# A transformer step in one kernel: no weight tasks in a unit's short last block, and a pace of 54 slots in place of 58

## The chip, the cores and the metric

The kernel runs on one core of a Trainium2 chip. The metric is the time of one execution on the device, in microseconds (us). A core has a matmul engine (PE), a vector engine (DVE), a scalar engine (ACT), GpSimd (POOL) and SyncE (SP), which here issues most of the DMAs. Each engine works off its own list of instructions in order; semaphores make one wait for another.

## The reference

Attention with a block mask feeds a layer of 8 experts with soft weights, and that feeds a gated layer:

```
attn = softmax(mask(q k^T / 8)) v                 # 4 batches x 8 heads, 576 positions of 64
x = attn as 2304 rows of 512
P = exp(x w_gate - max); 8 times: rows and columns of P are normed in turn
out = sum over e of P[:, e] * (relu(x w1[e]) w2[e])      # 8 experts, 512 -> 1024 -> 512
result = (silu(out wg) * (out wv)) wo                    # 512 -> 1536 -> 512
```

## The kernel before, in words

The experts are worked off as 16 units (half of an expert's hidden width each). The 2304 rows lie in two halves of 1152, and every product of a unit is done by a scheme of seven products of blocks in place of eight (Strassen's, in Winograd's form), each of them in three f16 products of high and low parts. A half's 1152 rows are cut in blocks of 256, 256, 256, 256 and 128, so a unit has four full blocks and a short one (`blocks`, `NB` = 5, `TB` = 256).

`products_in` issues the seven products of a block into three PSUM banks a, b and c in the order b c b a b c b. It yields after every half product: a full block takes 14 slots, a short one 7 (a short block's product is not halved). One `yield` is one slot of the planner. In the slot the main loop (`for _ in in_stream()`) also pulls one piece of an output product (`products_out`, lines 632 to 670, evacuated by ACT at lines 1427 and 1447 through `take`), and calls `background()`. The fifth product, S3, leaves its sum in bank b, where DVE's add of line 559 reads it; the seventh, X22, is written to the same bank, so PE waits for that add. DVE's adds of line 704 and subtractions of lines 193 and 680 make the low and high parts of the hidden activations (`sums_out`, `operand`), ACT's casts of line 683 the high parts.

Background tasks prepare the weights: those of the next expert unit (`expert_items`) and a share of those of the gated layer (`glu_items`). A task is some instructions: a maximum (line 375 or 437, DVE), a spread of it over the partitions (line 103 on DVE, 110 on PE, 116 on DVE) and the scale behind it (lines 155 to 163), a split in high and low parts (line 178 on ACT and 182 on DVE) with a subtraction of two quarters (line 303, DVE). They are queued in `bg`, and `bg.step()` issues one, or two light ones. `bg.load` fetches the next item's data ahead of it.

`background()` is asked once a slot. `todo` is the count of tasks left; `pace` holds the count at the unit's start and the slot it was taken in; `late` is `todo` less what a straight line down to zero would have left. Two tests follow each other, so up to two steps may be made in a slot: a step is made if `late` is above `most`, or above `-ahead` while `given`, a running sum of DVE work, is low. What is left at a unit's end stands in the queue when the next unit adds its own; `bg.until` forces tasks out if the weights a unit needs aren't made.

What is called a unit's first, second, third or fourth block below are its full ones. Tasks in a short block stand on DVE and ACT between the block's own instructions, in the order in which the slots issue them.

Of the kernel before, what the change touches and what calls it, by code (L numbers as in the profile page):

```python
# [30 lines left out]
def attention_moe_glu_kernel(  # L31
# [37 lines left out]
    TB = 256  # L69
    NU = E * FF // FU  # L70
    NG = F2 // FU
    blocks = [(c, min(TB, NH - c)) for c in range(0, NH, TB)]
# [435 lines left out]
    def later(d, f):  # L508

        due.setdefault(clock[0] + d, []).append(f)  # L510
# [160 lines left out]
    def operand(h, o, name, n, src, func=AF.Copy):  # L671

        h[o] = places.take(f"{name}_h{o}")
        hi, lo, src = h[o][:, 0, :, :n], h[o][:, 1, :, :n], src[:, :, :n]
        if func == AF.Relu:
            nc.scalar.activation(hi, src, AF.Relu)  # L676

            def cut_lo():
                given[0] += n
                nc.vector.scalar_tensor_tensor(lo, src, 0.0, hi, op0=ALU.max, op1=ALU.subtract)  # L680

            return cut_lo
        nc.scalar.copy(hi, src)  # L683
        if o in POOL_LO:
            return lambda: nc.gpsimd.tensor_tensor(lo, src, hi, op=ALU.subtract)

        def plain_lo():
            given[0] += n
            half_lo(lo, src, hi)

        return plain_lo
# [3 lines left out]
    def sums_out(h, name, n, x11, x12, x21, x22, spare, relu):  # L695


        los = {}

        def plus(o, x, y, op):  # L700
            o, x, y = (z[:, :, :n] for z in (o, x, y))
            given[0] += n
            if relu:
                nc.vector.scalar_tensor_tensor(o, x, 0.0, y, op0=ALU.max, op1=op)  # L704
            else:
                nc.vector.tensor_tensor(o, x, y, op=op)

        def step1():
            plus(spare, x22, x21, ALU.add)
            plus(x21, x11, x21, ALU.subtract)  # L710
            places.give(x22)

        def step2():
            los[S1] = operand(h, S1, name, n, spare)
            los[S3] = operand(h, S3, name, n, x21)
            plus(x11, x11, spare, ALU.subtract)

        def step3():
            los[S1]()
            los[S3]()  # L720
            places.give(spare, x21)
            los[S2] = operand(h, S2, name, n, x11)
            plus(x12, x12, x11, ALU.add)

        def step4():
            los[S2]()
            places.give(x11)
            los[S4] = operand(h, S4, name, n, x12)

        def step5():  # L730
            los[S4]()
            places.give(x12)

        for d, f in enumerate((step1, step2, step3, step4, step5)):
            later(d + 2, f)
# [3 lines left out]
    def expert_in(u, b, bank):  # L739

        h = hts[u, b] = {}
        n = blocks[b][1]
        name = f"m{u}_{b}"
        q = {}

        def plain(t, half, src, spare):
            h[t, half] = places.take(f"{name}_h{t}{half}")
            hi, lo = h[t, half][:, 0, :, :n], h[t, half][:, 1, :, :n]
            s = src[:, :, :n]
            if spare is not None:  # L750
                places.give(spare)

            def first():
                nc.scalar.activation(hi, s, AF.Relu)
                later(1, rest)

            def rest():
                nc.vector.scalar_tensor_tensor(lo, s, 0.0, hi, op0=ALU.max, op1=ALU.subtract)  # L758
                if (t, half) != (1, 0):
                    places.give(src)  # L760

            if (t, half) == (1, 1):
                later(3 if n == TB else 1, first)
            else:
                first()

        def quad(t, half, src, spare):
            q[t, half] = src
            if spare is not None:
                q["spare"] = spare  # L770
            if (t, half) == (1, 0):
                r = places.take(f"{name}_r", F32)
                nc.scalar.activation(r[:, :, :n], src[:, :, :n], AF.Relu)
                sums_out(h, name, n, q[0, 0], q[0, 1], r, q[1, 1], q["spare"], True)
                return
            o = {(0, 0): X11, (0, 1): X12, (1, 1): X22}[t, half]
            later(3 if o == X22 and n == TB else 2, lambda: later(1, operand(h, o, name, n, src, AF.Relu)))

        yield from products_in(name, b, units[u][0], bank, plain if u < 2 else quad, b == NB - 1)
# [481 lines left out]
    with tc.manual_schedule():  # L1261
# [123 lines left out]
        slots, ready_at, outs = [0], {}, set()  # L1385
# [69 lines left out]
        def out_stream(items, make):  # L1455

            for it in items:
                while ready_at.get(it, slots[0] + 1) > slots[0]:
                    yield False
                yield from make(*it)  # L1460
                outs.add(it)

        def in_stream():
            for u, b in seq:
                if u and b == (NEARLY if u < 2 else 0):
                    bg.until((u, 0))
                    if 2 <= u < NU - 1:
                        n = -(-sum(len(i[2]) for i in glu) // (NU - 1 - u))
                        share = []
                        while glu and n >= len(glu[0][2]) * 0.6:  # L1470
                            share.append(glu.popleft())
                            n -= len(share[-1][2])
                        if u == NU - 2:
                            share.extend(glu)
                            glu.clear()
                        i1, i2 = expert_items(u + 1)
                        bg.add(share[:-2] + [i1] + share[-2:] + [i2])
                        pace[:] = [sum(len(i[2]) for i in bg.items) + len(bg.now), slots[0]]
                yield from expert_in(u, b, bank)
                ready_at[u, b] = slots[0] + LAG  # L1480

# [150 lines left out]
        def glu_out(t, b):  # L1632
            def take(i, tk, cols, ps, what=None):
                if tk is None:
                    return
                x = tk * NI + i
                a = acc[:, x, cols]
                first = t == 0 and (x, cols.start) not in begun
                begun.add((x, cols.start))
                if first:  # L1640
                    nc.scalar.activation(a, ps, AF.Copy, scale=sos[b][:, t : t + 1])
                else:
                    nc.vector.scalar_tensor_tensor(a, ps, sos[b][:, t : t + 1], a, op0=ALU.mult, op1=ALU.add)
                count[x] = count.get(x, 0) + 1
                if count[x] == 3 * NG:
                    for g in range(4):
                        r0 = (4 * i + g) * CB + tk * HB
                        nc.sync.dma_start(out[r0 : r0 + HB, :], acc[g * HB : (g + 1) * HB, x])

            yield from products_out(f"go{t}_{b}", b, hts.pop((t, b)), gw[t, "o"], m, mdone, take, b == NB - 1)  # L1650
# [4 lines left out]
        def prep_stream():  # L1655
            for b in range(NB):
                while (NU - 1, b) not in outs:
                    yield False
                yield from x2_prep(b)
                prepped.add(b)  # L1660
# [9 lines left out]
        prepped = set()  # L1670
        seq3 = seq + [(NU + t, b) for t in range(NG) for b in range(NB)]
        xstream = prep_stream()
        pace = [0, 0]
        ostream = out_stream(seq3, lambda u, b: expert_out(u, b) if u < NU else glu_out(u - NU, b))
        credit = [0]

# [6 lines left out]
        def background():  # L1683


            given[0] = max(0, given[0] - 480)
            for ahead, room, most in ((6, 200, 6), (-2, 100, 11)):
                todo = sum(len(i[2]) for i in bg.items) + len(bg.now)
                late = todo - pace[0] * (1 - (slots[0] - pace[1]) / 58)
                if late > most or late > -ahead and given[0] < room:  # L1690
                    bg.step()

        for _ in in_stream():
            slots[0] += 1
            pull(1)
            if slots[0] % 2 == 0:
                next(steps, None)
            if routed and unscaled and (unscaled[0] % NI * P < blocks[NEARLY][0] or (1, NB - 1) in outs):
                scale_acc()
            next(xstream, None)  # L1700
            background()
            if len(made) == 2 * NU and places.spare(1):
                load_next()
# [50 lines left out]
```

## Time and profile before

| | us |
|---|---|
| median of 3 runs | 2087.34 |
| lowest and highest | 2084.76, 2088.24 |
| span of the profiled execution | 2083.4 |
| PE busy | 1949.0 (94%) |
| DVE busy | 1620.1 (78%) |
| ACT busy | 1379.9 (66%) |

The profile gives the execution's span, from its first to its last instruction, and no other time of it. The attention part ends before 400 us, the expert units run to about 1660, and the gated layer to the end. In the expert units PE is busy for 90% or more of every slice, and DVE between 80% and 90% of most.

### The profile page before, as it was taken

Reading aid. Unit: us, or ns where it says so; the run is one execution under the profiler, and the core shown is the slowest. Engines: PE = TensorE matmul, PEld = TensorE weight load, DVE = VectorE, ACT = ScalarE, POOL = GpSimd, SP = SyncE. Lnnn points to the kernel's source line nnn. Section 1 sums busy time; section 2 is a strip of 40 time slices with the busy share of each in tenths; the row PEclk is TensorE's granted clock in tenths of the full one; section 3 lists DMA queues with packets and bytes.
Section 4 is the critical chain, followed back from the end, with each engine's and each line's share of the span. In section 5 each row is a group of like instructions: output and inputs, shape, how many; then the busy total and the mean of one; then the engine's idle time right before and its main releaser. Section 6 shows DMA issues by size and latency. Waiting matters only on the chain.

```text
span 2083.4 us, 47251 instructions
## 1 busy us (share of the span) xinstructions
PE 1949.0 (94%) x18378; PEld 1672.9 (80%) x18378; DVE 1620.1 (78%) x3455; ACT 1379.9 (66%) x2940; POOL 612.8 (29%) x873
## 2 busy tenths in 40 slices
PE   6789899799999999999999999999999988999998
PEld 3457676698888888888888888888888877988887
DVE  7887765668787887978878788888887877666666
ACT  5665766348777777878777777777776566544442
POOL 4534444102333333333332333333332123000000
PEclk9889999999999999999999999999999999999999
DMA  5433331306687866878668786777877100301112
GB/s 155 112 96 105 84 105 49 122 22 122 120 172 155 172 136 125 178 150 171 132 132 179 149 178 134 153 157 144 180 148 168 37 11 1 87 21 37 47 42 52
DMA packets 168721, 236.41 MB, mean 113 GB/s; under 512 B 16432, under 2 KB 85680, under 8 KB 168496
## 3 DMA queue, kind: packets, MB, share of 16 engines
q0 software_dynamic: 66560, 107.37, 30.8%
q1 hardware_dynamic: 101936, 126.01, 19.9%
q8 instruction: 144, 2.36, 0.5%
q14 instruction: 81, 0.66, 0.1%
HBM read 90.98 MB, written 24.38 MB: 55 GB/s over the span
## 4 chain that ended last, share of the span: by engine, by line
PE 55%; DVE 15%; ACT 5%; DMA 3%; issue 3%; SPq 0%; POOL 0%; ACTq 0%; DVEq 0%
PE abc_m_b L537 11%; PE m_o_b L645 11%; PE m_o_ac L645 8%; PE abc_m_c L537 5%; PE abc_m_a L537 3%; PE abc_v_b L537 3%; PE abc_g_b L537 3%; PE m_go_b L645 3%; PE m_go_ac L645 2%; DVE m_t L704 2%; DVE m_h L193 2%; DMA wr<-in_w_dram 2%; PE abc_v_c L537 1%; DVE w L182 1%; PE abc_g_c L537 1%
## 5 line engine op out<-in xcount | busy, mean ns | idle before, releaser
L537 PEld LDWEIGHTS <-w 128*128 128x128 f16 x6720 | 609.8, 98 | 110.9 <-issue 45.7
L645 PEld LDWEIGHTS <-m_h 128*128 128x128 f16 x5292 | 514.0, 98 | 69.0 <-issue 10.5
L537 PE MATMUL abc_m_b<-xs,w 128*128 128x256 f16 (+1 forms) x3840 | 476.6, 264 | 31.9 <-DVE m_t L559 29.4
L1443 POOL DMA_DIRECT2D acc<-ev x351 | 305.4, 895 | 581.3 <-ACT ev L1447 367.4
L645 PE MATMUL m_o_b<-w,m_h 128*128 128x256 f16 x3024 | 403.5, 273 | 7.9 <-ACT ev L1447 7.7
L645 PE MATMUL m_o_ac<-w,m_h 128*128 128x256 f16 x2268 | 309.4, 273 | 0.4 <-ACT ev L1447 0.4
L537 PE MATMUL abc_m_c<-xs,w 128*128 128x256 f16 (+1 forms) x1920 | 230.7, 263 | 2.2 <-DVE m_h L758 1.6
L1447 ACT ACTIVATE ev<-m_o_b,pe 128x256 f32<-128x256 f32 x351 | 161.7, 476 | 64.0 <-PE m_o_b L645 52.8
L1447 ACT ACTIVATE ev<-m_o_ac,pe 128x256 f32<-128x256 f32 (+1 forms) x234 | 135.7, 580 | 47.8 <-PE m_o_ac L645 46.4
L178 ACT ACTIVATE w<-wr,ws 128x512 f16<-128x512 f32 x210 | 150.5, 723 | 12.7 <-DVE ws L163 10.3
L182 DVE SCALAR_TENSOR_TENSOR w<-wr,ws,w 128x512 f16<-128x512 f32 x210 | 155.5, 747 | 1.4 <-ACT w L178 1.4
L1431 POOL DMA_DIRECT2D acc<-ev_s x65 | 73.6, 1132 | 259.1 <-ACT ev_s L1427 259.1
L683 ACT CAST m_h<-m_t 128x512 f16<-128x512 f32 (+1 forms) x210 | 121.8, 580 | 41.2 <-DVE m_t L704 40.3
L676 ACT ACTIVATE m_h<-m_t 128x512 f16<-128x512 f32 (+1 forms) x210 | 121.8, 582 | 35.8 <-DVE m_t L574 24.9
L193 DVE TENSOR_TENSOR m_h<-m_t,m_h 128x512 f16<-128x512 f32 (+1 forms) x210 | 133.1, 635 | 8.7 <-ACT m_h L683 8.4
L680 DVE SCALAR_TENSOR_TENSOR m_h<-m_t,m_h 128x512 f16<-128x512 f32 (+1 forms) x210 | 132.2, 635 | 5.8 <-ACT m_h L676 5.6
L537 PEld LDWEIGHTS <-gg_w 128*128 128x128 f16 x1260 | 113.5, 98 | 22.2 <-issue 10.7
L996 POOL TENSOR_SCALAR e<-e,r 128x64 f32<-128x64 f32 (+2 forms) x144 | 78.1, 548 | 166.8 <-DVE r L991 111.9
L645 PEld LDWEIGHTS <-g_h 128*128 128x128 f16 x1134 | 111.0, 99 | 18.9 <-issue 5.4
L537 PEld LDWEIGHTS <-gv_w 128*128 128x128 f16 x1260 | 113.6, 98 | 13.2 <-issue 1.7
L537 PE MATMUL abc_m_a<-xs,w 128*128 128x256 f16 (+1 forms) x960 | 117.5, 262 | 0.0
L375 DVE TENSOR_REDUCE wmx<-wr 128x1 f32<-128x512 f32 x128 | 85.7, 679 | 15.0 <-DMA wr<-in_w_dram 14.9
(298 smaller groups left out, 3364.0 us busy)
## 6 DMA issues: line engine op xcount, KB each, us to landing
acc<-ev POOLq DMA_DIRECT2D x351, 256.0 KB, 4.3
wr<-in_w_dram SPq DMA_DIRECT2D x128, 256.0 KB, 4.8
acc<-ev_s POOLq DMA_DIRECT2D x52, 256.0 KB, 4.3
st<-hl SPq DMA_DIRECT2D x48, 144.0 KB, 3.6
raw_g<-in_w_gate_dram SPq DMA_DIRECT2D x12, 512.0 KB, 5.5
raw_v<-in_w_val_dram SPq DMA_DIRECT2D x12, 512.0 KB, 4.5
raw_o<-in_w_out_dram SPq DMA_DIRECT2D x12, 512.0 KB, 5.0
scr_g<-gg SPq DMA_DIRECT2D x21, 256.0 KB, 2.9
```

Of the source, the lines that this page charges most:

```text
L178: nc.scalar.activation(hi, src, AF.Copy, scale=s)
L182: nc.vector.scalar_tensor_tensor(lo, src, s, hi, op0=ALU.mult, op1=ALU.subtract)
L193: nc.vector.tensor_sub(lo, src, hi)
L375: nc.vector.tensor_reduce(g["mx"][:, k : k + 1], g["b"][k // 2][k % 2], axis=AX.XY, op=ALU.max, apply_absolute_value=True)
L537: nc.tensor.matmul(ps[:, f], W[o][:, sh, k, f * P : (f + 1) * P], xs[:, o, mh, k, c0 : c0 + n], start=x not in begun, stop=True, skip_grou ...
L645: nc.tensor.matmul(ps, h[o][:, sh, k, ii * P : (ii + 1) * P], W[o][:, mh, k], start=o in (X11, X12) and k == 0 and j == 0, stop=True, skip ...
L676: nc.scalar.activation(hi, src, AF.Relu)
L680: nc.vector.scalar_tensor_tensor(lo, src, 0.0, hi, op0=ALU.max, op1=ALU.subtract)
L683: nc.scalar.copy(hi, src)
L996: nc.gpsimd.tensor_scalar(et[c][:, :n], et[c][:, :n], g["r"][:, c : c + 1], 1.0, op0=ALU.mult, op1=ALU.mult)
L1443: nc.gpsimd.dma_start(acc[:, x], e, accum_op=ALU.add)
L1447: nc.scalar.activation(e[:, cols], ps, AF.Copy, scale=p)
```

## The change

`short[0]` is set when a unit's block is begun, true for the block of 128 rows; `background()` returns at once while it is true. The straight line of the pace reaches zero 54 slots after the unit's start, and not 58. Nothing else differs, and no instruction is new.

```diff
--- before.py
+++ after.py
@@ -1476,6 +1476,7 @@
                         i1, i2 = expert_items(u + 1)
                         bg.add(share[:-2] + [i1] + share[-2:] + [i2])
                         pace[:] = [sum(len(i[2]) for i in bg.items) + len(bg.now), slots[0]]
+                short[0] = blocks[b][1] < TB
                 yield from expert_in(u, b, bank)
                 ready_at[u, b] = slots[0] + LAG
 
@@ -1670,7 +1671,7 @@
         prepped = set()
         seq3 = seq + [(NU + t, b) for t in range(NG) for b in range(NB)]
         xstream = prep_stream()
-        pace = [0, 0]
+        pace, short = [0, 0], [False]
         ostream = out_stream(seq3, lambda u, b: expert_out(u, b) if u < NU else glu_out(u - NU, b))
         credit = [0]
 
@@ -1684,9 +1685,11 @@
 
 
             given[0] = max(0, given[0] - 480)
+            if short[0]:
+                return
             for ahead, room, most in ((6, 200, 6), (-2, 100, 11)):
                 todo = sum(len(i[2]) for i in bg.items) + len(bg.now)
-                late = todo - pace[0] * (1 - (slots[0] - pace[1]) / 58)
+                late = todo - pace[0] * (1 - (slots[0] - pace[1]) / 54)
                 if late > most or late > -ahead and given[0] < room:
                     bg.step()
```

The first place is DVE's list in the short block of unit 6 (its weight tasks are unit 7's, `w_7`), around the add of line 559 into which bank b (`abc_m_4_b`; 4 is the block) is summed. Before:

```order
L193 TENSOR_TENSOR m_3_h_12550<-m_3_t_12348,m_3_h_12550 128x512
L182 SCALAR_TENSOR_TENSOR w_7_0_12532<-wr_1_00_12300,ws_1_12523,w_7_0_12532 128x512
L303 TENSOR_TENSOR wr_1_00_12300<-wr_1_01_12302,wr_1_00_12300 128x512
L182 SCALAR_TENSOR_TENSOR w_7_1_12554<-wr_1_10_12304,ws_1_12523,w_7_1_12554 128x512
L303 TENSOR_TENSOR wr_1_01_12302<-wr_1_11_12306,wr_1_01_12302 128x512
L559 TENSOR_TENSOR m_4_t_12609<-m_4_t_12506,abc_m_4_b 128x2x128
L193 TENSOR_TENSOR m_3_h_12571<-m_3_t_12317,m_3_h_12571 128x512
L574 TENSOR_TENSOR m_4_t_12546<-m_4_t_12546,abc_m_4_c 128x2x128
```

After:

```order
L704 SCALAR_TENSOR_TENSOR m_3_t_12351<-m_3_t_12351,m_3_t_12274 128x512
L193 TENSOR_TENSOR m_3_h_12525<-m_3_t_12274,m_3_h_12525 128x512
L193 TENSOR_TENSOR m_3_h_12527<-m_3_r,m_3_h_12527 128x512
L704 SCALAR_TENSOR_TENSOR m_3_t_12320<-m_3_t_12320,m_3_t_12351 128x512
L193 TENSOR_TENSOR m_3_h_12554<-m_3_t_12351,m_3_h_12554 128x512
L559 TENSOR_TENSOR m_4_t_12605<-m_4_t_12523,abc_m_4_b 128x2x128
L193 TENSOR_TENSOR m_3_h_12573<-m_3_t_12320,m_3_h_12573 128x512
```

One pair of 182 and 303 is left out here, and the other has moved to an earlier place, ahead of the block before's three 704s; `w_7_1` is made in unit 7.

The second place is DVE's list in the fourth block of unit 7, around its add of line 559 (`abc_m_3_b`). The `gv` are splits of the gated layer's weights. Before:

```order
L103 TENSOR_SCALAR w_d<-ident,wm_8_1_13628 128x128
L182 SCALAR_TENSOR_TENSOR gv_2_13605<-f_v_11_13399,gs_v_13533,gv_2_13605 128x512
L303 TENSOR_TENSOR f_v_11_13399<-f_v_11_13399,f_v_00_12309 128x512
L182 SCALAR_TENSOR_TENSOR gv_4_13625<-f_v_00_12309,gs_v_13533,gv_4_13625 128x512
L303 TENSOR_TENSOR f_v_10_13338<-f_v_10_13338,f_v_11_13399 128x512
L559 TENSOR_TENSOR m_3_t_13694<-m_3_t_13565,abc_m_3_b 128x512
L680 SCALAR_TENSOR_TENSOR m_3_h_13675<-m_3_t_13654,m_3_h_13675 128x512
L182 SCALAR_TENSOR_TENSOR gv_6_13664<-f_v_01_12885,gs_v_13533,gv_6_13664 128x512
L182 SCALAR_TENSOR_TENSOR gv_5_13686<-f_v_11_13399,gs_v_13533,gv_5_13686 128x512
L574 TENSOR_TENSOR m_3_t_13616<-m_3_t_13616,abc_m_3_c 128x512
L182 SCALAR_TENSOR_TENSOR gv_3_13707<-f_v_10_13338,gs_v_13533,gv_3_13707 128x512
```

After:

```order
L193 TENSOR_TENSOR m_2_h_13576<-m_2_t_13331,m_2_h_13576 128x512
L182 SCALAR_TENSOR_TENSOR gv_2_13562<-f_v_11_13382,gs_v_13495,gv_2_13562 128x512
L303 TENSOR_TENSOR f_v_11_13382<-f_v_11_13382,f_v_00_12266 128x512
L182 SCALAR_TENSOR_TENSOR gv_4_13596<-f_v_00_12266,gs_v_13495,gv_4_13596 128x512
L303 TENSOR_TENSOR f_v_10_13323<-f_v_10_13323,f_v_11_13382 128x512
L182 SCALAR_TENSOR_TENSOR gv_6_13635<-f_v_01_12936,gs_v_13495,gv_6_13635 128x512
L182 SCALAR_TENSOR_TENSOR gv_5_13653<-f_v_11_13382,gs_v_13495,gv_5_13653 128x512
L559 TENSOR_TENSOR m_3_t_13702<-m_3_t_13573,abc_m_3_b 128x512
L680 SCALAR_TENSOR_TENSOR m_3_h_13683<-m_3_t_13661,m_3_h_13683 128x512
L182 SCALAR_TENSOR_TENSOR gv_3_13673<-f_v_10_13323,gs_v_13495,gv_3_13673 128x512
L116 TENSOR_REDUCE w_r<-m_w_13663 128x1
```

Two splits, `gv_6` and `gv_5`, stand ahead of the add where they stood behind it. The short block's add of this unit is the same row of DVE's list before and after.

## Rows read from the trace of the kernel before

**Rows 1.** The page's head, and PE's granted clock in 40 slices (tenths).
```profile
span 2083.4 us, 47251 instructions
...
PEclk9889999999999999999999999999999999999999
```

**Rows 2.** Windows: span, busy PE, PEld, DVE, ACT, POOL (instructions), clock, DMA share, GB/s.
```profile
935.10:955.20 20.10, 18.45 (x166) 15.91 (x164) 19.68 (x38) 16.63 (x33) 6.50 (x8) 1.00 0.78 172
956.50:967.60 11.10, 9.63 (x128) 8.75 (x126) 10.82 (x24) 10.52 (x24) 3.47 (x4) 1.00 1.00 207
...
1041.90:1052.80 10.90, 9.46 (x128) 8.82 (x127) 10.69 (x19) 9.86 (x22) 3.47 (x4) 1.00 0.74 123
...
1107.80:1126.10 18.30, 18.30 (x170) 16.39 (x169) 16.38 (x28) 13.81 (x28) 6.35 (x8) 1.00 1.05 255
```

**Rows 3.** Table of waits: engine, line, waited for, us in total, times, longest.
```profile
PE abc_m_b L537 <- DVE m_t L559: 29.4, 15, 6.2
```

**Rows 4.** Timeline (start, length, engine, line, idle before): PE's waits, units 0, 2, 14.
```profile
396.33 3.71 PE L537 MATMUL abc_m_b<-xs,w 128*128 128x256 f16 x24 [6.17 <-DVE m_t L559]
...
412.11 0.83 PE L537 MATMUL abc_m_b<-xs,w 128*128 128x128 f16 x12 [3.67 <-DVE m_t L559]
...
534.29 0.83 PE L537 MATMUL abc_m_b<-xs,w 128*128 128x128 f16 x12 [1.81 <-DVE m_t L559]
...
1571.14 0.83 PE L537 MATMUL abc_m_b<-xs,w 128*128 128x128 f16 x12 [1.34 <-DVE m_t L559]
```

**Rows 5.** Timeline of PE and DVE in unit 6's short block.
```profile
874.21 0.83 PE L537 MATMUL abc_m_b<-xs,w 128*128 128x128 f16 x12
...
875.72 0.74 DVE L182 SCALAR_TENSOR_TENSOR w<-wr,ws,w 128x512 f16<-128x512 f32 x1
...
876.20 0.82 PE L645 MATMUL m_o_ac<-w,m_h 128*128 128x256 f16 x6
...
876.50 0.69 DVE L303 TENSOR_TENSOR wr<-wr,wr 128x512 f32<-128x512 f32 x1
...
877.11 0.74 DVE L182 SCALAR_TENSOR_TENSOR w<-wr,ws,w 128x512 f16<-128x512 f32 x1
...
877.77 0.68 DVE L303 TENSOR_TENSOR wr<-wr,wr 128x512 f32<-128x512 f32 x1
...
878.37 0.41 DVE L559 TENSOR_TENSOR m_t<-m_t,abc_m_b 128x256 f32<-128x256 f32 x1
...
878.71 0.68 DVE L193 TENSOR_TENSOR m_h<-m_t,m_h 128x512 f16<-128x512 f32 x1
...
878.84 0.83 PE L537 MATMUL abc_m_b<-xs,w 128*128 128x128 f16 x12 [1.82 <-DVE m_t L559]
```

**Rows 6.** Timeline of DVE, ACT and PE in unit 13's fourth block.
```profile
1457.72 0.75 DVE L182 SCALAR_TENSOR_TENSOR go<-f_o,gs_o,go 128x512 f16<-128x512 f32 x1
...
1458.39 0.69 DVE L303 TENSOR_TENSOR f_o<-f_o,f_o 128x512 f32<-128x512 f32 x1
...
1459.59 0.69 DVE L193 TENSOR_TENSOR m_h<-m_r,m_h 128x512 f16<-128x512 f32 x1
...
1460.19 0.69 DVE L704 SCALAR_TENSOR_TENSOR m_t<-m_t,m_t 128x512 f32<-128x512 f32 x1
...
1460.91 0.62 ACT L683 CAST m_h<-m_t 128x512 f16<-128x512 f32 x1 [1.80 <-DVE m_t L704]
...
1461.44 0.83 ACT L1447 ACTIVATE ev<-m_o_b,pe 128x256 f32<-128x256 f32 x2
...
1461.95 0.82 PE L645 MATMUL m_o_b<-w,m_h 128*128 128x256 f16 x6 [1.75 <-ACT ev L1447]
```

**Rows 7.** Timeline of PE and DVE in unit 7's fourth block.
```profile
945.68 0.82 PE L645 MATMUL m_o_b<-w,m_h 128*128 128x256 f16 x6 [0.99 <-ACT ev L1447]
...
950.31 0.46 PE L110 MATMUL m_w<-w_d,ones 128*128 128x128 f32 x2 [0.54 <-DVE w_d L103]
...
952.73 0.68 DVE L559 TENSOR_TENSOR m_t<-m_t,abc_m_b 128x512 f32<-128x512 f32 x1
...
953.88 0.82 PE L537 MATMUL abc_m_b<-xs,w 128*128 128x256 f16 x6
```

## The prediction

> **What bounds the kernel now.** I read the page's busy shares first, then the table of waits, then the timeline of TensorE (PE) alone, and last the timeline of all engines around each gap. From about 440 to 1640 us the kernel runs the expert units, and there TensorE is the bound: the granted clock stands at its highest digit in every slice after the first four [rows 1] (1.00 in blocks of units 7 to 9, so the 2.4 GHz level), and a full block of 14 slots takes 18.30 us in which PE is busy for all 18.30 [rows 2], so a slot is 1.31 us. Time is lost only where PE stands still. The table of waits has one entry that is large and repeats: PE's products into bank b waiting for the vector engine's (DVE's) add of line 559, 15 times, 29.4 us together [rows 3]. Two of the 15 lie in unit 0, 6.17 and 3.67 us. The other 13 are one per unit, units 2 to 14, always before the last product of the short block, 1.81 us in the first and 1.34 in the last [rows 4]; together 29.4 - 6.17 - 3.67 = 19.6 us. In order they are 1.81, 1.81, 1.34, 1.43, 1.82, 1.34, 1.43, 1.82, 1.34, 1.44, 0.80, 1.80 and 1.34.
>
> How one comes about is seen in unit 6 [rows 5]. The fifth product (S3) starts at 874.21 and lasts 0.83, so its sum can be added from about 875.1. DVE gets to the add at 878.37, since from 875.72 it works off two pairs of weight tasks, 182 and 303, that stand ahead of it in its order. PE's work before the seventh product ends at 876.20 + 0.82 = 877.02, and the product starts at 878.84. Without the two pairs the add would start at 875.72 and PE would find it done. In the short block a slot is no longer than elsewhere, but product and add follow two slots apart in place of four or five. The room is 877.02 - 875.1 less the add's 0.41, 1.5 us of queue on DVE; in a full block it is one slot more, less the longer add, 2.6.
>
> **What a queue is made of.** An instruction on 512 columns is shown as 0.69 us long, a 182 as 0.75, but the next starts 0.60 and 0.67 us after it [rows 6], and after a 256-column add 0.34. I count with these steps: I went through DVE's order slot by slot, added the steps and took 1.31 off per slot; what is left over is the queue. On the kernel before this gives 1.7 to 3.7 us of queue ahead of the short block's add, so 0.2 to 2.2 us of wait against 0.80 to 1.82 measured. That is good to about half a microsecond, one unit apart: unit 3, where it gives least and 1.81 was measured, since DVE stood waiting for a transfer there.
>
> The Trainium skill speaks to this choice: "Perfetto Trace Analysis", section "Per-instruction lifecycle", says that the shown window of a DVE instruction runs until its write is acknowledged, while the next may start to fetch when the execution is over. By the shown lengths the short blocks of before would have waited 2 to 3 us each, near twice what was measured, so the steps stand.
>
> **The change, part by part.** No instruction is added or taken away; tasks move. (1) In the short block no weight task is issued, so DVE's work there falls from 10.5 to 12.1 us (by steps, in 9.17 us of slots; the trace shows 10.69 and 10.82 busy in units 8 and 7 [rows 2]) to 6.0. (2) The 7 or 8 tasks go into the four full blocks, through the pace of 54 slots, and 8 or 9 tasks of a unit's supply (1 to 5 before) are left for the next unit's first block. That block, in units 3 to 14, had DVE at 53 to 61% by steps and gets 62 to 69%: it costs nothing. None is left for the forced loop at a unit's start or at its first output: both find their weights made.
>
> The units fall into three kinds that repeat.
> - Units 2, 5, 8, 11: the full blocks' DVE load stays at or below 0.90 of the slots; the queue ahead of the short add falls from 3.0 (unit 2: 3.7) to 0.5 us, below 1.5. Their waits go: 1.81 + 1.43 + 1.43 + 1.44 = 6.1 us.
> - Units 3, 6, 9, 12, 13: the third block rises from 0.83-0.90 to 0.97 (13: 1.02), but the queue is drained before the short add, 0.2 to 0.4 us, in unit 13 1.6. Their waits (1.81 + 1.82 + 1.82 + 0.80 + 1.80) go but for 0.1: 7.9 us.
> - Units 4, 7, 10, 14: the second block comes to 1.04 and the fourth, 1.04 before, to 1.09. The short add stands behind as much work as before (it is the same row of DVE's order), with 2.7 us of queue against 2.6. Their four waits of 1.34 stay.
>
> **What the moved tasks cost.** PE waits in full blocks by another way, seen in unit 13 [rows 6]: DVE's queue delays the 704 at 1460.19, the scalar engine (ACT), in order, waits 1.80 for it with its cast of line 683, behind that cast stands the evacuation of line 1447, and PE's next output product waits for that one, 1.75 us. The queue there, at the second or fourth block's start, was 5.1 us; unit 9 had 3.3 at that place and lost nothing. Interpolated: nothing below 3.3, one us more of wait per us of queue. After the change the queue there is 4.0 to 4.3 in units 3, 6 and 9: 0.7 each, 2.1. In unit 13 it is 5.2, as before, and a second place at 4.2 adds 0.9. In the kind of unit 7 it is 4.2 once and 3.9 once: 0.9 + 0.6; these units had already 0.99 and 0.54 [rows 7], and their fourth block's add, which had 953.88 - 952.73 - 0.68 = 0.47 us to spare [rows 7], now stands behind two more 182s (1.33) and takes perhaps 0.4. But a stall of PE lets DVE catch up, and so the short block's wait shrinks by about what the earlier ones grew; I take their sum, 2.87 per unit, as unchanged (from 1.3 less to 2.5 more, times four). Bounds for all of these places: from 0 (unit 9 before) to 1.75 (unit 13 before) each. I take 2.1 + 0.9 = 3.0.
>
> **Unit 0 and 1.** The short block of unit 0 has four pairs and three maxima ahead of its add, some 6.9 us, all moved out: 3.67 us go. They land in unit 1's first block: 19 tasks where 7 were, a queue of about 3 us, over the 2.6 for line 559 by 0.4 and in front of the last relu (line 758), whose bank the next block's product wants a slot later, some 2 us; nothing like it was lost there before. Bounds 0 and 3.7; I take 2.4, a net gain of 1.3.
>
> **Sum.** 6.1 + 7.9 - 3.0 + 0 + 1.3 = 12.3 us off the profiled span of 2083.4 us, so 2071.1. The page gives no time of that execution beside its span; the three timed runs are 2084.76 to 2088.24, so about 4 us lie around the span or between executions. I take the 12.3 off the median: 2075.0 us. The attention part before and the gated part after it hold the same instructions in the same order; the first block of unit 15 gets four tasks more at a DVE load of 0.62.
>
> **Rivals.**
> - All cover holds: the queues drain a little faster than I count (half a microsecond, the error above), no new wait arises, and the four 1.34s shrink too. Ceiling 19.6 + 3.7 = 23 us: 2064. For it: DVE often waits for PE in full blocks of before; against: fourth blocks over 1.0. Chance 0.12.
> - Half of it is given back: new waits of 1.2 to 1.7 at the ten or so places: 4 to 8 us saved, 2079 to 2083. Chance 0.16.
> - The waits only move: if an instruction held DVE for its whole shown length (0.69 and 0.75), DVE would be over 1.0 in nearly every third and fourth block, the four short adds would wait 2.8 us more each (11 us), and gain and loss cancel: 2083 to 2091. Against it: the counted waits of before. Chance 0.14.
> - Slower: the in-order ACT chain of unit 13 (683 behind 704, 1447 behind both) at all twelve places where DVE's queue rises over 3.3, with the queue at each passing its 5.1: 12 x 1.75 = 21 plus 2.4 in unit 1, against 6.1 + 7.9 + 3.7 = 17.7 gained: 5.7 us more, 2093. It decides if the queue there passes 5 us, 0.8 to 1.2 above my count. Chance 0.07.
> - The change doesn't do what it says, the tasks being forced in one burst at the unit's start: the order shows them spread over the first block, so 2087; chance 0.01.
>
> **The numbers.** The forecast, 2071 to 2079, has 0.50. A difference below 0.2% (4.2 us) can't be told from none. Faster: 0.50 + 0.12 + 0.16 = 0.78; same 0.14; slower 0.08. The range for 8 in 10 is 2068 to 2086: it leaves out most of the ceiling and the slower case; the forecast's own range is 2071 to 2079.
>
> **What would show it.** Right: PE's waits for line 559 fall from 15 to about 6, 29.4 us to about 12 (6.17 of unit 0 stays); the short blocks of units 2, 3, 5, 6, 8, 9, 11 and 12 last 9.2 us; units 4, 7, 10 and 14 still wait there or, for the same sum, earlier. New waits for line 1447 of under 1 us stand near the fourth block's start of units 3, 6 and 9. Wrong: waits of PE for line 1447 or line 559 in full blocks that sum to over 10 us, or short blocks that still wait in the first two kinds.

## The result and the profile after

The change made the kernel slower: 2111.9 us against 2086.1 (medians), a ratio of 1.0123 (95% interval 1.0109 to 1.0137), about 26 us. One of the four timed runs of the changed kernel was slow (4040 us) and stands outside the ratio, though it counts in this median; the other three took 2110.85 to 2112.87. The forecast was 2075, its range for 8 in 10 ended at 2086, and its slowest rival stood at 2093. The profiled execution has a span of 2109.1 us where [rows 1] has 2083.4, so its 25.7 us are the same loss, and it can be read from the trace.

The page's head of the changed kernel, and the granted clock in 40 slices:

```profile
span 2109.1 us, 47276 instructions
...
PEclk9889999899999999999999999999999999999999
```

From its table of waits (engine, line, waited for, us in total, times, longest):

```profile
PE abc_m_b L537 <- DVE m_t L559: 28.9, 11, 5.7
...
DVE wmx L375 <- DMA wr<-in_w_dram: 17.2, 13, 3.4
PE m_o_b L645 <- ACT ev L1447: 17.0, 18, 1.7
...
ACT f_o L456 <- DMA raw_o<-in_w_out_dram: 11.2, 3, 5.2
ACT f_v L456 <- DMA raw_v<-in_w_val_dram: 11.1, 3, 4.6
...
ACT f_g L456 <- DMA raw_g<-in_w_gate_dram: 9.2, 3, 5.1
```

PE's wait for line 559 is as long in sum as in [rows 3], and that hides everything: none of the 13 short blocks waits for it any more, and eight full blocks do, 2.03 to 3.70 us each, 21.9 together. Line 1447 went from 7.7 us to 17.0. The four rows of DVE and ACT are the ones that the prediction left out: they wait for loads (DMA). Before, the same rows were a fifth shorter in sum, and that of line 1447 less than half as long:

```profile
DVE wmx L375 <- DMA wr<-in_w_dram: 14.9, 12, 3.9
...
ACT f_v L456 <- DMA raw_v<-in_w_val_dram: 8.7, 3, 3.8
...
ACT f_o L456 <- DMA raw_o<-in_w_out_dram: 8.2, 3, 4.2
...
PE m_o_b L645 <- ACT ev L1447: 7.7, 11, 1.8
...
ACT f_g L456 <- DMA raw_g<-in_w_gate_dram: 7.5, 3, 4.7
```

Two kinds of load are meant. A weight item of an expert is fetched by four DMAs into `wr`, and its first tasks are the four maxima of line 375. A gated item is fetched as 64-bit words into the tile `raw`, which has one buffer; ACT reads it in line 456, DVE shifts the result in line 461 and reads `raw` again up to line 471, and only then can the next `raw` load start.

What matters is what stands behind the waiting instruction in its engine's order. Unit 9's fourth block, changed kernel, timeline (start, length, engine, line, idle before):

```profile
1133.34 2.68 SPq L370 DMA_DIRECT2D wr<-in_w_dram  x4
...
1137.26 0.69 DVE L375 TENSOR_REDUCE wmx<-wr 128x1 f32<-128x512 f32 x1 [0.90 <-DMA wr<-in_w_dram]
...
1140.26 2.02 DVE L375 TENSOR_REDUCE wmx<-wr 128x1 f32<-128x512 f32 x3 [2.31 <-DMA wr<-in_w_dram]
...
1142.71 0.68 DVE L559 TENSOR_TENSOR m_t<-m_t,abc_m_b 128x512 f32<-128x512 f32 x1
...
1143.44 0.82 PE L537 MATMUL abc_m_b<-xs,w 128*128 128x256 f16 x6 [2.85 <-DVE m_t L559]
```

All four maxima stand ahead of the add, DVE idles 0.90 and 2.31 us for the transfer, and PE waits 2.85. The same place before:

```profile
1118.07 1.97 SPq L370 DMA_DIRECT2D wr<-in_w_dram  x4
...
1121.67 0.69 DVE L375 TENSOR_REDUCE wmx<-wr 128x1 f32<-128x512 f32 x1 [1.05 <-DMA wr<-in_w_dram]
1122.28 0.68 DVE L559 TENSOR_TENSOR m_t<-m_t,abc_m_b 128x512 f32<-128x512 f32 x1
...
1124.81 0.69 DVE L375 TENSOR_REDUCE wmx<-wr 128x1 f32<-128x512 f32 x1 [0.66 <-DMA wr<-in_w_dram]
```

One maximum ahead of the add, three behind; the transfer is waited for as well, but PE never notices. In unit 7 it is the raw load. Changed kernel:

```profile
947.77 0.66 ACT L456 ACTIVATE f_v<-raw_v 128x512 f32<-128x512 f32 x1 [4.37 <-DMA raw_v<-in_w_val_dram]
...
948.47 0.43 DVE L461 TENSOR_SCALAR f_v<-f_v 128x512 int32<-128x512 int32 x1 [4.45 <-ACT f_v L456]
...
949.54 0.68 DVE L559 TENSOR_TENSOR m_t<-m_t,abc_m_b 128x512 f32<-128x512 f32 x1
...
950.27 0.81 PE L537 MATMUL abc_m_b<-xs,w 128*128 128x256 f16 x6 [2.14 <-DVE m_t L559]
```

Before, the add of that block stood ahead of the shift, with one instruction (line 680) between them:

```profile
928.66 0.37 SPq L428 DMA_DIRECT2D raw_v<-in_w_val_dram  x1
...
929.71 0.69 DVE L559 TENSOR_TENSOR m_t<-m_t,abc_m_b 128x512 f32<-128x512 f32 x1 [0.40 <-PE abc_m_b L537]
...
933.31 0.66 ACT L456 ACTIVATE f_v<-raw_v 128x512 f32<-128x512 f32 x1 [3.78 <-DMA raw_v<-in_w_val_dram]
...
934.00 0.43 DVE L461 TENSOR_SCALAR f_v<-f_v 128x512 int32<-128x512 int32 x1 [3.00 <-ACT f_v L456]
```

Windows of units 6 and 7, each its four full blocks and then its short one, changed kernel (span, busy PE, PEld, DVE, ACT, POOL, clock, DMA share, GB/s), and below the same units before:

```profile
803.17:884.16 80.99, 76.41 (x685) 67.60 (x683) 64.29 (x120) 59.72 (x118) 25.55 (x28) 0.98 0.74 158
884.16:892.95 8.79, 8.79 (x124) 8.36 (x122) 7.95 (x14) 7.17 (x18) 3.47 (x4) 1.00 0.74 126
892.95:974.17 81.22, 77.10 (x684) 67.57 (x683) 67.01 (x126) 60.16 (x120) 25.80 (x28) 0.98 0.71 147
974.17:983.35 9.18, 9.10 (x124) 8.34 (x122) 9.08 (x17) 8.28 (x19) 3.50 (x4) 1.00 0.99 200
```

```profile
794.18:868.48 74.30, 74.30 (x683) 66.63 (x682) 59.28 (x109) 56.75 (x112) 25.61 (x28) 1.00 0.79 167
868.48:879.67 11.19, 9.37 (x126) 8.62 (x124) 10.88 (x26) 9.77 (x22) 3.53 (x4) 1.00 0.75 132
879.67:956.50 76.83, 75.18 (x684) 66.78 (x683) 64.25 (x119) 58.56 (x116) 25.59 (x28) 1.00 0.73 151
956.50:967.16 10.66, 9.19 (x124) 8.36 (x122) 10.42 (x23) 10.08 (x23) 3.47 (x4) 1.00 1.04 215
```

Unit 6's short block, whose wait [rows 5] show, fell from 11.19 us to 8.79, its four full blocks rose from 74.30 to 80.99; 4.6 of the 6.7 are idle PE, and 2.1 are longer busy time for the same products, most of it at a lower clock (the last section shows the stretch). DVE is busy for 64.29 of the 80.99.

### The profile page after: what moved, and what is told of

Read it like the earlier page. It is cut to its first block, busy times and chain, and to the rows that moved or that the text cites. A ratio compares the mean times of both kernels' runs of the same rounds, so it can differ in the third digit from the quotient of the medians.

```text
span 2109.1 us, 47276 instructions
## 1 busy us (share of the span) xinstructions
PE 1961.2 (93%) x18378; PEld 1679.2 (80%) x18378; DVE 1624.4 (77%) x3455; ACT 1378.4 (65%) x2940; POOL 614.2 (29%) x873
## 4 chain that ended last, share of the span: by engine, by line
PE 53%; DVE 16%; ACT 4%; DMA 4%; issue 3%; SPq 0%; POOL 0%; DVEq 0%; ACTq 0%
PE m_o_b L645 11%; PE abc_m_b L537 11%; PE m_o_ac L645 8%; PE abc_m_c L537 5%; PE abc_m_a L537 3%; PE abc_v_b L537 3%; PE abc_g_b L537 3%; PE m_go_b L645 3%; PE m_go_ac L645 2%; DVE m_t L704 1%; PE abc_v_c L537 1%; DVE w L182 1%; PE abc_g_c L537 1%; DVE m_h L680 1%; DMA wr<-in_w_dram 1%
```

## The experiments

All are against runs of the kernel before on the same chip. A = units 3, 6, 9, 12, 13; B = 4, 7, 10, 14; C = 2, 5, 8, 11; these are the three kinds of units that the prediction names.

**One part of the change at a time.**

```diff
 e1:  - late = todo - pace[0] * (1 - (slots[0] - pace[1]) / 54)
      + late = todo - pace[0] * (1 - (slots[0] - pace[1]) / 58)
 e2:  - if short[0]:
      -     return
```

> The return in the short block alone, the pace back at 58 slots. Theory (order behind a load): the changed kernel loses since DVE works in order and instructions that wait for a transfer (the first weight maxima, line 375, or the shift of line 461 behind ACT's line 456) now stand ahead of the full block's add of line 559, on which PE waits 2.0 to 3.7 us in nine places. With the pace of 58 the order puts unit 6's maxima in slots 53 to 55, behind the add of slot 51, and unit 7's second shift in slot 40, behind the add of slot 37; only unit 12 keeps a shift ahead of it. So those waits and the clock they cost go, the short blocks' gain of some 20 to 25 us stays, ACT's in-order waits of 1.0 to 1.7 may stay: 2069 to 2082 us, faster than both kernels. Rival (full blocks overfilled): the moved tasks bring DVE over the slots' time in the third and fourth blocks wherever they stand; the same tasks are moved here, so most of the loss stays: 2095 to 2110 us.

Measured: 2109.8 us, ratio 1.0102 (1.0080 to 1.0125). The forecast missed by 28 us, and the time lies in the rival's range, full blocks overfilled; e4 below tests that reason. The waits did leave line 559, as the order said, but not PE: unit 7 in e1,

```profile
940.26 0.37 SPq L428 DMA_DIRECT2D raw_v<-in_w_val_dram  x1
...
945.04 0.66 ACT L456 ACTIVATE f_v<-raw_v 128x512 f32<-128x512 f32 x1 [4.55 <-DMA raw_v<-in_w_val_dram]
...
946.70 0.59 ACT L773 ACTIVATE m_r<-abc_m_b 128x512 f32<-128x512 f32 x1
...
947.33 1.63 PE L537 MATMUL abc_m_c<-xs,w 128*128 128x256 f16 x12 [2.11 <-ACT m_r L773]
```

The load is waited for 4.55 us by ACT itself, and behind line 456 stands line 773, which empties a bank that PE wants. In units 5, 8 and 11 it is line 562 (1.5 to 1.8 us), in unit 12 line 559 (4.17). So not one add but anything behind a load's wait is at risk.

> The pace of 54 slots alone, tasks allowed in the short block as before. Theory (order behind a load): the pace is what puts the load-bound instructions ahead of the add: unit 6's four maxima in slots 48 to 51 ahead of the add of slot 51, unit 7's second shift in slot 34 and first maximum in slot 37 ahead of the add of slot 37. The waits of 2 to 3 us in full blocks are there, ACT's too, and only part of the short blocks' waits goes: 2100 to 2118 us. Rival (full blocks overfilled): fewer tasks are pushed into the full blocks than in the changed kernel, some stay in the short one, so the loss is at most a third of its 25 us: 2083 to 2095 us.

Measured: 2109.7, ratio 1.0113 (1.0090 to 1.0137), the time that the theory had. Its places are the theory's only in part: full blocks of units 3, 6, 9 and 13 wait for line 559 (0.65 to 3.89 us), but those of units 4, 7 and 10 for line 1447 (2.56 each). Either part alone loses nearly as much as both (23 us against 26), so the loss is no sum of two prices: each moves tasks by itself, and the order before hid more of its loads than either.

**Loads without the waits.** e3 gives loads out two items ahead; e4 leaves the later raw loads out and keeps the tasks in their slots; e5 does both, e6 both in the kernel before.

```diff
 e3:  - bg, glu = Background(1), deque()
      + bg, glu = Background(2), deque()
 e4:  - raw = rawp.tile([P, 2, TB], I64, tag="raw", ...)
      + once = not rawp1
      + if once:
      +     rawp1.append(rawp.tile([P, 2, TB], I64, tag="raw", name="raw_one"))
      + raw = rawp1[0]
 ...
      - nc.sync.dma_start(raw, ...)
      + if once:
      +     nc.sync.dma_start(raw, ...)
```

> The changed kernel with loads given out two items ahead in place of one; the tasks keep nearly the same slots (the maxima of units 6 and 9 the same ones, 49 to 51), but the weight block's load is issued some 14 slots before its first maximum in place of 4. The raw tile has one buffer, so its load can't be earlier. Theory (order behind a load): the maxima find their data; the waits of the full fourth block in units 3, 6, 9, 13 (3.70, 2.93, 2.85, 2.03 us) go, with 1 to 2 us of lower clock behind each; those behind the raw load in units 4, 7, 10, 14 (2.90, 2.14, 2.37, 2.97) and 12 (3.02) stay: 2093 to 2102 us. Rival (full blocks overfilled): the same instructions stand in the same slots, so the add is as late: within 4 us of the changed kernel's 2112.

> The changed kernel in which the gated layer's 64-bit weights are fetched once into the raw tile and all later loads of it are left out, so that every gated weight block is made from the same block of w_gate; every instruction of the engines stands where it was. Theory (order behind a load): ACT's line 456 never waits, and the waits of 2.90, 2.14, 2.37, 2.97 us in units 4, 7, 10, 14 and 3.02 in unit 12 go with the clock they cost; those behind the weight loads in units 3, 6, 9, 13 stay or shrink by up to 1 us, since the queue has 35 transfers less: 2092 to 2100 us. Rival (full blocks overfilled): the add is late by DVE's own work, within 4 us of the changed kernel's 2112.

Measured: e3 2101.0 (1.0075, 1.0051 to 1.0098), 11 below the changed kernel, in the theory's range. e4 2083.0 (0.9988, 0.9976 to 1.0000), 29 below, more than the 12 to 20 expected. In e4 the waits for line 559 in units 4, 7, 10 and 14 are gone, and so is that of 3.02 us for line 562 in unit 12; those of units 3, 6, 9, 13 stay (3.01, 3.06, 2.86, 1.19). In e3 it is the other way round (the raw waits are there, now in front of line 1447 too). DVE holds the same instructions in e4 as in the changed kernel, so an overfilled DVE isn't the cause of those waits.

> The changed kernel with both edits at once: loads two items ahead, and the raw tile fetched once (the later raw loads left out, so the gated weights are wrong). Theory (order behind a load): the two parts of the loss lie in different units and add up. Alone the one took 11 us off the changed kernel's 2112 and the other 29; the weight-load waits of units 3, 6, 9, 13 that are left in the second (3.0, 3.1, 2.9, 1.2 us and the clock behind them, 12 us in all by the four stretches of full blocks) go as well: 2068 to 2076 us, some 10 to 18 below the kernel before, which is about what the prediction gave the change. Rival (full blocks overfilled): what is left of the loss after the raw loads is DVE's own work, and the loads two ahead add nothing: 2080 to 2086.

> The kernel before with the same two edits (the later raw loads left out, loads two items ahead). Theory (order behind a load): before, the same loads were waited for as long (ACT's line 456 up to 4.71 us, the maxima up to 1.49) but nothing that PE needs stood close behind, so taking the waits away gives little: 2080 to 2088 us, within 6 of the kernel before. Rival (less traffic helps anything): leaving out the raw loads speeds up the kernel by itself, and the 29 us were not the changed kernel's loss: 2055 to 2070.

Measured: e5 2067.2 (0.9912, 0.9891 to 0.9933), just under the theory's range: the two edits take 45 us off the changed kernel. But e6 is 2064.4 (0.9896, 0.9873 to 0.9919): they take some 22 off the kernel before as well, not 6 at most, and that is the range of the rival, by which less traffic helps anything. These two runs can't tell the waits from the traffic; e7 and e14 below, with every transfer made, can for some units. Units 6 and 7 of e6, then the full blocks of e5 (same columns):

```profile
789.64:864.00 74.36, 74.36 (x684) 66.63 (x682) 60.92 (x113) 57.58 (x115) 25.55 (x28) 1.00 0.73 148
864.00:874.23 10.23, 9.21 (x126) 8.62 (x124) 9.27 (x21) 8.95 (x20) 3.51 (x4) 1.00 0.79 131
874.23:948.75 74.52, 74.52 (x685) 66.87 (x683) 65.02 (x121) 60.09 (x118) 25.56 (x28) 1.00 0.72 144
948.75:958.63 9.88, 8.95 (x124) 8.36 (x122) 9.64 (x21) 9.29 (x21) 3.48 (x4) 1.00 0.89 161
```

```profile
788.68:865.65 76.97, 75.05 (x686) 66.78 (x683) 64.00 (x120) 59.60 (x118) 25.50 (x28) 1.00 0.71 143
...
874.43:951.20 76.77, 75.12 (x685) 66.67 (x683) 66.83 (x126) 60.41 (x120) 25.78 (x28) 1.00 0.69 141
```

With no load to wait for, the kernel before has no stall in unit 7's full blocks (74.52 where it had 76.83), and the waits of [rows 7], 0.99 for line 1447 and 0.54 for `w_d`, are gone: they came behind the 3.78 us that ACT had waited for `raw`. Its short blocks shrink too, 11.19 to 10.23 and 10.66 to 9.88. And the change, seen without loads, gains nothing: 2067.2 against 2064.4, with intervals that overlap.

**Each part without loads.** e1 and e2 with the two edits of e5.

> The return alone (pace 58) with loads two items ahead and the later raw loads left out (the gated weights are wrong). With no load to wait for, what is left of the return is the gain in the short blocks against what the moved tasks cost in the full ones. Theory (the change's full-block cost comes mostly from the pace): the line of 58 slots packs the full blocks less, so their new waits behind ACT's line 1447 are half of those with 54: 2058 to 2063 us, below the kernel before under the same two edits (2064). Rival (it comes from the moved tasks, wherever the line ends): 2065 to 2069, as the whole change under the same edits (2067).

> The pace of 54 alone with loads two items ahead and the later raw loads left out (the gated weights are wrong). Theory (the full-block cost comes mostly from the pace): the full blocks pay as in the whole change, near 20 us against the kernel before under these edits, and the short blocks gain only a third: 2070 to 2080 us. Rival (it comes from the moved tasks of the short block): few are moved here, so 2062 to 2067.

Measured: e9 2070.4 (0.9933, 0.9915 to 0.9950), e12 2073.9 (0.9947, 0.9928 to 0.9965), 6 and 9.5 over e6 (e9's interval just overlaps e6's). The theory of e9 is wrong: the return with the old pace gains nothing either, and lies a little over its rival's range; e12 fell where the theory had it, but by luck: its full blocks pay 7.2 us over e6 in place of near 20, and its short blocks, which were to gain a third, lose 2.8. Set against e1 and e2, the two edits take off 39 us with the return alone and 36 with the pace alone, where it was 22 for the kernel before and 45 for the whole change. By the trace the return's cost lies mostly in A's full blocks (12.9 us over e6, behind line 1447, 1.2 to 2.4 a time), the pace's in B's (8.4). So both parts make full blocks dearer without any load, in different units.

**Units 0 and 1.**

```diff
 e13: - short[0] = blocks[b][1] < TB
      + short[0] = u > 1 and blocks[b][1] < TB
```

> The changed kernel, but the return holds from unit 2 on only; units 0 and 1 hand out tasks in their short blocks as before. Theory (the first block of unit 1 can't take unit 0's moved tasks): the waits of 1.1 and 3.0 us in unit 1 go, unit 0's 3.7 comes back, and units 0 and 1 end as early as before: 2105 to 2109 us, 3 to 6 below the changed kernel. Rival (the prediction's count, a net gain of 1.3 there): 2112 to 2115.

Measured: 2105.1 (1.0091, 1.0068 to 1.0115), 7 under the changed kernel and in the theory's range. In the trace unit 1's short block is back from 14.30 us to 9.47 and unit 2's short block starts 3.7 earlier; but the whole profiled execution is only 2.9 us shorter than the changed kernel's, so what else the 7 may hold isn't seen there.

**Nothing left out, raw loads apart.** In B and C two gated items follow each other, and the second one's load can't start before line 471 of the first. e7 (changed kernel) and e8 (return alone) put the second weight item between them; e10 (before) and e11 (return alone) choose, of all places for the two weight items, the one with the fewest such pairs; e14 (before) does as e7, with `if u < 11 and`, so up to unit 10. All give loads out two ahead.

```diff
 e7, e8, e14:
- bg.add(share[:-2] + [i1] + share[-2:] + [i2])
+ tail = [share[-2], i2, share[-1]] if len(share[-2][2]) == 4 else share[-2:] + [i2]
+ bg.add(share[:-2] + [i1] + tail)
 e10, e11:
+ def bad(x, u=u):
+     return sum(len(p[2]) < 5 and q[0] == 0 for p, q in zip(x, x[1:]))
...
+ bg.add(min(ways, key=lambda w: (bad(left + w[0]), w[1]))[0])
```

> Nothing left out. The changed kernel with loads two items ahead, and in a unit whose last but one gated item is a short one (4 tasks) the second weight item put between the last two gated items, so that two raw loads no longer follow each other (but at the start of unit 13). Theory (order behind a load): each raw load is issued a whole weight item before it is used, its wait goes without leaving out a transfer, and the short blocks' gain stays: 2068 to 2084 us, less than before and near the version without raw loads. Rival (full blocks overfilled, or the tasks in new slots stand ahead of other work): 2092 to 2110.

> As e7_order, with the pace of 58 slots (the return in the short block alone). Theory (order behind a load): the return alone lost 23 us because its loads were waited for at other places of the block (line 773 and line 562 in place of line 559); with the waits gone it gains as e7_order does: 2066 to 2084 us. Rival (full blocks overfilled): as without the order, 2100 to 2112.

> Nothing left out: the kernel before (no return, pace 58) with loads two items ahead, and the two weight items put among the gated ones where the fewest raw loads follow a short gated item. Theory (load waits cost the kernel before some 20 us as well, as leaving the raw loads out showed): no wait for a raw load is left near PE's path but one in unit 14, so it comes near that version: 2064 to 2074 us, the fastest that computes everything. Rival (the 21 us were the transfers' own traffic, not the waits): within 5 us of before, 2081 to 2090.

> As e10_before_order, with the return in the short block. Theory (load waits): against e8_order_return_only (2080) the waits for raw loads in units 12 and 13 go, 2.2 + 2.5 us and what follows them: 2070 to 2078. What it lies above or below e10_before_order is the price of the return when loads aren't waited for; expected 0 to 8 above, since full blocks pay more than short ones gain. Rival (the return pays once loads don't matter): 2 or more below e10_before_order.

> Nothing left out: the kernel before (no return, pace 58) with loads two items ahead, and in units up to 10 the second weight item between the last two gated items where the first of them is short; units 11 to 14 in the old order. Theory (waits for loads): units 4, 7 and 10 lose their waits as in e10_before_order, 3.4 us each and part of the short blocks' waits; units 12 and 14 are as before: 2068 to 2075 us, the fastest that computes everything. Rival (e10's 7 us were all there is, its loss in units 14 and 15 comes from elsewhere): 2077 to 2081.

Measured: e7 2091.7 (1.0031, 1.0014 to 1.0048), e8 2079.8 (0.9973, 0.9962 to 0.9985), e10 2079.2 (0.9975, 0.9965 to 0.9985), e11 2086.4 (1.0007, 0.9995 to 1.0018), e14 2075.4 (0.9949, 0.9929 to 0.9969). e8 is as forecast; e7, e10 and e11 are not as fast as forecast, and e14 is just over; e7 is 0.3 us from its rival's range. Where raw loads are apart, the units are free of their cost with every transfer made: e14's unit 7,

```profile
872.38:946.68 74.30, 74.30 (x683) 66.64 (x681) 58.77 (x110) 57.16 (x113) 25.69 (x29) 1.00 0.70 137
```

74.30 where the kernel before had 76.83 and e6, with fewer transfers, 74.52. That settles waits against traffic for the B units of the kernel before. For the changed kernel e7 does: its full blocks of units 3, 4, 6, 7, 9 and 10 take 76.3 to 77.4 us with every transfer made, near e5's 76.8 to 77.0, where the changed kernel's take 79.4 to 82.0.

Most misses lie where items still follow each other or come late: e10 and e11 lose 9 and 16 us against e6 in unit 14's full blocks, where two short gated items in a row and then a late weight item are waited for (ACT 5.05 and DVE 3.15 in e10); e14 has a raw wait of 4.45 in unit 11, which costs 4.2. e7's miss is only in part of that kind. Against the kernel before, its full blocks lose 5.2 and 4.6 us in units 12 and 13, where raw loads are waited for 4.31 and 4.51. But they also lose 3.1 in each of units 3, 6, 9 (two waits of 0.9 behind line 1447 and longer products), 2.7 in each of units 5, 8, 11 (1.6 behind the same line) and 4.1 in unit 15, and no load is waited for there. Tasks in new slots ahead of other work were its rival's reason.

e14 is faster than both kernels, 12 us under the kernel before, with an interval clear of 1. It changes the order and the lead of the loads together; to which of the two a unit owes its gain isn't shown.

## Why the prediction was wrong

Each stretch from the traces, us: what was predicted, what the change did, and what it did with no load waited for (e5 less e6).

| | predicted | after less before | e5 less e6 |
|---|---|---|---|
| unit 0's short block | -3.7 | -2.1 | -2.2 |
| unit 1 | +2.4 | +5.6 | +5.6 |
| short blocks, C | -6.1 | -6.8 | -6.7 |
| short blocks, A | -7.9 | -11.6 | -4.5 |
| short blocks, B | 0 | -6.0 | -3.0 |
| full blocks, C | 0 | +1.7 | -0.3 |
| full blocks, A | +3.0 | +27.1 | +10.2 |
| full blocks, B | 0 | +18.1 | +9.2 |
| sum | -12.3 | +26.0 | +8.3 |

- "Their waits go" was right for both kinds, and B's went as well: a short block takes 8.8 to 9.2 us, as the steps on DVE had it. The gain behind the change was there, and larger than forecast: 24.4 us in the short blocks of the three kinds for 14.0. With no load waited for it is 14.2, which meets the 14.0 by luck: A gives 4.5 where 7.9 were counted, and B 3.0 where none was.
- The step that failed is "What the moved tasks cost", 3.0 us; the full blocks of A and B paid 45.2. It counted DVE's queue in steps and took each task to be ready when its turn comes. The first tasks of an item aren't: their load is issued 3 or 4 slots earlier, 3.9 to 5.2 us, and the four DMAs of unit 9 took 6.9 us from 1133.34 to the three maxima at 1140.26, the raw load of unit 7 before 4.65 from 928.66. Moving tasks moved these waits in front of lines 559, 562 and 1447. The experiments show the size: the two edits that take these waits away gain 45 us in the changed kernel (e5) and 22 in the kernel before (e6).
- The rows had it. The transfer that DVE waited for was named in the prediction, for unit 3, and set aside as the exception of one unit; and [rows 7]'s 0.99 and 0.54 were read as the queue's, though 3.78 us of ACT's waiting stood ahead of them. The interpolation itself had one end that was no load's: unit 13's 1.75 is still 1.69 in e6.
- Also within that step, the queue's part was too small: without loads the full blocks of A and B pay 19.4 us, 2.2 to 2.7 a unit but for unit 12, where 0 to 1.5 were given. With unit 1's 5.6 that more than cancels what the short blocks gain, as in the rival "the waits only move", which had 0.14, but not by its reason: no short add waits longer, and in e5 none waits. The rival "slower" named the right engines and the wrong cause: line 1447 rose by 9 us, not by its 21.
- Units 0 and 1: unit 0's gain is there (-2.1 for -3.7); unit 1 pays 5.6 for 2.4. PE waits 1.11 us for line 559 in its full block and 3.04 for line 758 in its short one, which takes 14.30 us in place of 9.47. e13 confirms that it comes from the return.
- The sign that the prediction named as its refutation, over 10 us of waits for lines 1447 or 559 in full blocks, is what the trace shows: 21.9 for line 559 alone.

Open: the change without loads costs 2.8 us by the medians and 8.3 by these stretches. Single executions differ in the attention part (unit 0's short block starts between 395.6 and 401.9 us over the profiles), and e6's starts 4.5 later than e5's, so more than "no gain" can't be said. Nor was it shown what, in the return alone, fills A's full blocks.

## What to carry to other kernels

Before you move work in an in-order list, mark each instruction that waits for a transfer, and look at what stands behind it before and after: such a wait costs nothing until something that the bound engine needs falls in behind it. A wait in the table of waits that PE doesn't feel is a price that any reordering can call in, so give the load a longer lead, or keep two users of one buffer apart, and only then tune the order. And judge a tuned order by taking the disputed waits away in both kernels: a gain against the kernel before may be the loads' and not the order's.

## What the runs showed of the hardware

A stall of PE can cost more than its length. Windows of the changed kernel behind three of them (2.93 us in unit 6, 2.85 in unit 9, 3.70 in unit 3; same columns):

```profile
615.40:619.00 3.60, 3.60 (x23) 2.82 (x23) 3.46 (x11) 3.25 (x6) 1.87 (x2) 0.68 0.19 28
619.00:622.00 3.00, 3.00 (x36) 2.71 (x34) 2.90 (x5) 2.21 (x5) 1.09 (x2) 0.81 0.90 143
...
879.80:883.00 3.20, 3.20 (x16) 2.34 (x16) 2.91 (x10) 1.62 (x4) 1.20 (x1) 0.51 0.10 15
...
1143.44:1147.00 3.56, 3.56 (x39) 3.28 (x39) 3.42 (x11) 3.22 (x6) 2.04 (x2) 1.00 0.23 37
```

After 2.93 us of idling the granted clock was 0.51, the 1.2 GHz level, for 3.2 us; after 2.85 it stayed at 1.00; after 3.70 it was 0.68 and then 0.81. Six products that take 0.82 us took 1.44 to 1.49 there. Over the full blocks of units 2 to 14 the change costs 46.8 us: 35.8 are idle PE and 11.0 are longer busy time for the same products, which no count of waits contains. The granted clock falls short of 1.00 there by 6.6 us in sum (one less the clock, times the length: an estimate from the windows of the full blocks), so not all of the 11.0 is the clock's.

The Trainium skill, "DMA: Bandwidth & Descriptors", section "Anatomy of one DMA — SWDGE (gpsimd) path", fits a DMA's time as 2.0 us plus its bytes over 436 GB/s, for the path that GpSimd issues; for a raw load of 512 KB that would be an estimate of 3.2 us. Here the loads are SyncE's and run beside other transfers, and from issue to use the trace has 4.65 us (unit 7 before) and 4.78 (e1). So the 3.2 is too short for these loads, and no run here shows why.
